# Attention and two feed-forward layers on one core: z and the memory matrices in one load per batch entry, and a new task order

## The chip, the cores and the metric

The kernel runs on one core of one Trainium2 chip. A core has five engines with instruction streams of their own: TensorE (PE; its weight loads are shown apart as PEld), VectorE (DVE), ScalarE (ACT), GpSimd (POOL) and SyncE (SP). SP does no arithmetic here; it issues nearly all the transfers between memory and the core, one after the other. The metric is the time of one execution on the device in microseconds (us), smaller is better.

## The reference

Three parts follow each other. B, H, S, D are 4, 8, 576, 64; M and z are a given memory of each head.

```
scores = q @ k^T / sqrt(D), causal;  a = softmax(scores);  local = a @ v
p = phi(q)                                  # elu(q) + 1
mem = (p @ M) / (p . z + 1e-6)
x = sigmoid(beta) * mem + (1 - sigmoid(beta)) * local     # [B, H, S, D] -> [B*S, H*D]
x = (silu(x @ w_gate) * (x @ w_val)) @ w_out              # 512 -> 1536 -> 512
x = bounded_square(x @ w_in) @ w_out2                     # 512 -> 2048 -> 512
```

## The kernel before

The work is written as tasks (engine, length, priority, what must be done before, which buffers it holds). A planner, `Plan.order`, walks through time with these lengths: whenever an engine is free, it takes the ready task with the lowest priority number whose buffers are free. The order that comes out is written down engine by engine, and on the chip each engine then follows its list strictly; a load that must wait on SP holds up all the loads behind it. There are two plans. The first holds the attention, the decoding of twelve weight tiles and the first products of the feed-forward layer (early units, `L1031`, tile `xh`). The second holds the rest.

The attention goes by pairs of heads: 16 pairs, four of each batch entry, each in `Attention.pair(b, n)`. For one pair the steps are these.

- SP loads `kn` (k, 4 issues: two of 128x4x64 and the two tails), `qn` (q, 3 issues), `vn` (v, 3 issues), z as `zb` (all partitions) and `zh` (two halves) with 3 issues, and the memory matrix `MZ` with 2 issues. `kn`, `vn`, `zb`, `MZ` have three buffers each.
- PE transposes k and q (`tk`, `tm`, `tq`), DVE or ACT copy them out, PE makes the scores (`s`, L611 and L641), DVE takes the maximum (L621, L648), ACT the exponential (L628, L659).
- POOL scales each block of `a` by its sum (L696). PE transposes it (`t`, L707, L730, L747), and DVE or ACT copy the result out as `R`.
- ACT and DVE make phi(q) as `p` (L530, L533, L537); POOL multiplies it by z (L542, L546), folds it (L553), and scales `p` by the norm (L563); PE transposes it (`tp`), and it is copied out as `P`.
- PE adds P @ M (L775) and R @ v (L782) in `av0` and `av1`. The result goes to `x`, and SP stores it.

POOL also does three of the steps of each weight tile (L875, L878, L911). The first early unit can run when a batch entry's first 512 tokens of `x` are stored and loaded again as `xh`.

The priorities are numbers in the tables `ORDER`, `FIRST_ORDER` (the first three pairs), `EARLY`, `GROUP_AT` and `X_AT`; `COPY` says which of DVE and ACT does a copy. The planner counts one issue on SP as 530 ns. Ahead of all, PE runs 16 products of zeros of 64 columns (`hold`, L1132).

The loads that the change touches:

```
def load_z():
    st["zb"] = self.bt.tile([P, 2, D], F32, name="zb", tag="zb")
    nc.sync.dma_start(
        st["zb"].rearrange("p h d -> p (h d)"),
        self.z[b, hs].rearrange("h d -> (h d)").partition_broadcast(P))
    st["zh"] = self.bt.tile([P, D], F32, name="zh", tag="zh")
    for h in range(2):
        nc.sync.dma_start(st["zh"][h * 64:(h + 1) * 64], self.z[b, 2 * n + h].partition_broadcast(64))

def load_M():
    for h in range(2):
        nc.sync.dma_start(MZ()[halves[h], h], self.M[b, 2 * n + h])
```

Of the kernel before, what the change touches and what calls it, by code (L numbers as in the profile page):

```python
# [9 lines left out]
F32 = mybir.dt.float32  # L10
# [20 lines left out]
FIRST_PAIRS = 3  # L31
AB, RB1, RB0 = 3, 2, 2
NOACT = 4
WARM = 16
AHEAD = 30
CUTS = (0, 2, 4)
EARLY = (35250.2957, 41308.3926, 11466.9687, 5162.3933, -48855.3305, 35090.3538, 21413.9511, 24260.6754, 7741.602, 20677.2758, 29371.8961, 20358.7385)
# [7 lines left out]
GROUP_AT, X_AT = (33565.3008, -22387.616, 43473.4923), (39993.454, 16553.201, -28923.1154)  # L45
# [10 lines left out]
HT = 512  # L56
# [8 lines left out]
    "load": -9480.7466, "load_v": 47393.1398, "load_z": -13855.6362, "load_M": 23016.7593, "tk": 27046.2635,  # L65
    "tm": -61762.0282, "tq": -17638.6547, "tk.cp": -18004.5022, "tm.cp": -2334.3136, "tq.cp": 3746.4569,
    "min": -8183.9045, "exp": -8979.6499, "phi": -13315.5241, "w": -36009.8218, "fold": -10020.024, "nrm":
# [9 lines left out]
}  # L77
FIRST_ORDER = {
    "load": -31396.1901, "load_v": 17116.4282, "load_z": -30006.9326, "load_M": 10452.2857, "tk": 47974.63,
    "tm": -14289.6988, "tq": -9446.1095, "tk.cp": -11189.0118, "tm.cp": -15504.3662, "tq.cp": 3520.7596,  # L80
    "min": -24283.9254, "exp": -25956.4452, "phi": 2222.4379, "w": -21034.9661, "fold": -31090.2871, "nrm":
# [9 lines left out]
}  # L91
COPY = {"tk": "ACT", "tm": "DVE", "tq": "ACT", "tp": "DVE", "tp4": "ACT", "t4": "ACT", "t03": "ACT", "t02": "DVE",
        "t01": "ACT", "t13": "DVE", "t12": "ACT", "t11": "ACT"}
# [13 lines left out]
class Plan:  # L107
# [38 lines left out]
    def dma(self, prio, times, fn, deps=(), uses=(), behind=None):  # L146

        t = self.add("SP", 530 * len(times), prio, fn, deps, uses, 0, behind)
        self.last = t
        return self.add("DMA", sum(times), prio, lambda: None, [t], uses)  # L150
# [85 lines left out]
    def emit(self, spare=None, place=None):  # L236

        end, todo = 0, self.order()
        until = max((t["at"] for t in todo if place in t["uses"]), default=0)
        for t in todo:
            if spare and t["eng"] == "PE":
                if end and t["at"] < until:
                    spare(t["at"] - end)
                end = t["at"] + t["dur"]
            t["fn"]()
# [57 lines left out]
class Attention:  # L306
# [3 lines left out]
    def __init__(self, ctx, tc, plan, q, k, v, M_prev, z_prev, beta, cst, xs):  # L310
        self.tc, self.nc, self.plan = tc, tc.nc, plan
        nc = tc.nc
# [3 lines left out]
        pool = lambda name, bufs: ctx.enter_context(tc.tile_pool(name=name, bufs=bufs))  # L316
        self.ld, self.bt, self.ph = pool("ld", 3), pool("bt", 3), pool("ph", 2)
# [3 lines left out]
        for tags, n in ((("kn", "qn", "vn", "zb", "K", "S", "P", "QZ", "MZ"), 3), (("a4",), 2),  # L321
                        (("a0", "a1", "a2", "a3"), AB), (("R1_0", "R1_1"), RB1),
                        (("R0_0", "R0_1"), RB0), (("e", "p", "x"), 2), (("mn",), 3), (("bank",), 8)):
            for t in tags:
                plan.cap(t, n)

        ac = self.ac
# [23 lines left out]
        self.spare = plan.inst("bank")  # L351
        for t in self.a4:
            nc.gpsimd.memset(t[:, S:640], 0.0)
        self.QZ, self.MZ = ([ac.tile([P, 2, D], F32, name=f"{x}_{i}") for i in range(3)] for x in ("QZ", "MZ"))
# [33 lines left out]
    def pair(self, b, n):  # L388
# [42 lines left out]
        i_k, i_q, i_v = pl.inst("kn"), pl.inst("qn"), pl.inst("vn")  # L431
# [24 lines left out]
        i_z, i_M = pl.inst("zb"), pl.inst("MZ")  # L456
        i_K, i_S, i_P, i_Q4 = pl.inst("K"), pl.inst("S"), pl.inst("P"), pl.inst("QZ")
        QZ, MZ = (lambda: self.QZ[i_Q4.slot]), (lambda: self.MZ[i_M.slot])

        def load_z():  # L460
            st["zb"] = self.bt.tile([P, 2, D], F32, name="zb", tag="zb")
            nc.sync.dma_start(
                st["zb"].rearrange("p h d -> p (h d)"),
                self.z[b, hs].rearrange("h d -> (h d)").partition_broadcast(P))
            st["zh"] = self.bt.tile([P, D], F32, name="zh", tag="zh")
            for h in range(2):
                nc.sync.dma_start(st["zh"][h * 64:(h + 1) * 64], self.z[b, 2 * n + h].partition_broadcast(64))

        def load_M():
            for h in range(2):  # L470
                nc.sync.dma_start(MZ()[halves[h], h], self.M[b, 2 * n + h])
# [14 lines left out]
        t_z = dma("load_z", [182, 91, 91], load_z, uses=[i_z])  # L486
        t_M = dma("load_M", [91, 91], load_M, uses=[i_M])


        def mk(kind, shape):  # L490
            if kind not in st:
                st[kind] = self.st.tile(shape, F32, name=kind, tag=kind)
            return st[kind]
# [45 lines left out]
        def f_w():  # L539
            w, p = st["e"], st["p"]  # L540
            zp = st["zb"]
            nc.gpsimd.tensor_mul(  # L542
                w[:, 0:8].rearrange("p (c h) d -> p c h d", h=2),
                p[:, 0:8].rearrange("p (c h) d -> p c h d", h=2),
                zp[:, None, :, :].to_broadcast([P, 4, 2, D]))
            nc.gpsimd.tensor_mul(w[:, 8], p[:, 8], st["zh"])  # L546
# [213 lines left out]
        def av(rg, deps):  # L760
# [3 lines left out]
            i_o = bank()  # L764
# [23 lines left out]
            def lo():  # L788
# [4 lines left out]
                    [i_o, i_P, i_v, i_M, *(i_R1, i_R0)[rg], *([self.spare] if num < FIRST_PAIRS else [])])  # L793
# [242 lines left out]
def tile_attention_two_moe(  # L1036
# [78 lines left out]
    with ExitStack() as actx:  # L1115
# [12 lines left out]
        def hold(n=WARM):  # L1128
            if "t" not in idle:
                idle["t"] = at.ps.tile([P, HT], F32, name="idle", tag=f"bank{at.spare.slot}")  # L1130
            for _ in range(n):
                nc.tensor.matmul(idle["t"][:, 0:P // 2], still, still[:, 0:P // 2], start=True, stop=True)  # L1132

        idle = {}
        plan.add("PE", 10, -2.0e6, hold, uses=[at.spare])
# [458 lines left out]
```

## Time and profile before

| | |
|---|---|
| median of 3 runs | 1071.93 us (1071.68 to 1072.39) |
| profiled execution, its own time | 1074.18 us |
| span of its profile | 1072.4 us |
| PE / PEld busy | 98% / 81% |
| DVE / ACT / POOL busy | 62% / 54% / 20% |
| granted clock of PE, mean | 0.992 |

The span is what the profiler recorded, and the execution's own time is 1.78 us longer. Busy shares are means over the whole span: POOL works in the attention alone, which is the first quarter. A busy PE is not PE at its peak, since the time of a product is that between its start and its modelled end, and products overlap. The granted clock is a share of 2.4 GHz; 0.50 is 1.2 GHz.

### The profile page before, as it was taken

To read this page: it belongs to the slowest core of one execution; us is meant where nothing else is said; L and a number is where in the kernel's file an instruction comes from. 1 tells how busy PE (TensorE), PEld (TensorE's weight loads), DVE (VectorE), ACT (ScalarE), POOL (GpSimd) and SP (SyncE) were. 2 spreads that over 40 slices of the span, in tenths; PEclk is the share of its full clock that TensorE was granted. 3 is DMA by queue.
4 is the path that set the end of the run, shared out by engine and by line. 5 is a ranking of instruction groups with operands and counts; after the bars stand their busy time and mean duration, and the time that the engine had idled before them with its cause. 6 is when DMAs were issued, how large, how long until landed. Compare 5 with 4: busy or idle time off the path is not lost.

```text
span 1072.4 us, 17753 instructions
## 1 busy us (share of the span) xinstructions
PE 1050.2 (98%) x6112; PEld 874.0 (81%) x6112; DVE 666.8 (62%) x1531; ACT 573.8 (54%) x1298; POOL 217.1 (20%) x302
## 2 busy tenths in 40 slices
PE   7989999999999999999999999899999999999998
PEld 6656667767779888889888888788899998899987
DVE  4868877773005787867877677653657577543443
ACT  6868788884212445535445444554555555444443
POOL 6979988993000000000000000000000000000000
PEclk9889999999999999999999999999999999999999
DMA  6577555334486879856985959899887987954522
GB/s 138 125 208 196 162 154 151 98 113 141 167 279 229 283 257 374 301 176 221 343 300 203 365 208 400 331 405 407 313 342 257 396 297 303 390 185 170 177 79 79
DMA packets 178025, 260.71 MB, mean 243 GB/s; under 512 B 74256, under 2 KB 102928, under 8 KB 177936
## 3 DMA queue, kind: packets, MB, share of 16 engines
q1 hardware_dynamic: 176030, 258.23, 69.4%
q10 hardware_dynamic: 1906, 1.35, 0.4%
q8 instruction: 49, 0.80, 0.3%
q14 instruction: 40, 0.33, 0.1%
HBM read 177.74 MB, written 81.79 MB: 242 GB/s over the span
## 4 chain that ended last, share of the span: by engine, by line
PE 93%; SPq 2%; DMA 2%; DVE 1%; ACT 1%; issue 0%; POOL 0%; ACTq 0%; DVEq 0%
PE mm L1031 28%; PE acc L1534 18%; PE mm L1283 16%; PE acc L1378 14%; PE av L782 4%; PE s L611 3%; PE t L730 2%; PE av L775 2%; PE s L641 1%; PE t L747 1%; PE t L707 1%; PE tp L569 1%; SPq L439 1%; DMA vn<-in_v_dram 0%; DMA raw<-in_moe_w_gate_dram 0%; PE tq L511 0%
## 5 line engine op out<-in xcount | busy, mean ns | idle before, releaser
L1534 PE MATMUL acc<-wu,h 128*128 128x512 f32 x864 | 211.9, 393 | 5.0 <-DVE h L1200 4.0
L1031 PE MATMUL mm<-xb,wu 128*128 128x512 f32 (+1 forms) x1008 | 201.3, 359 | 0.0
L1031 PEld LDWEIGHTS mm<-xb,wu 128*128 128x128 f32 x1008 | 170.0, 189 | 28.2
L1534 PEld LDWEIGHTS acc<-wu,h 128*128 128x128 f32 x864 | 157.6, 189 | 35.4 <-DVE h L1200 2.3
L1283 PE MATMUL mm<-xb,wu 128*128 128x256 f32 x1296 | 169.0, 284 | 0.6 <-ACT mm L1354 0.6
L1283 PEld LDWEIGHTS mm<-xb,wu 128*128 128x128 f32 x1296 | 164.9, 192 | 5.0 <-ACT mm L1354 1.0
L1378 PE MATMUL acc<-h,wu 128*128 128x512 f32 (+1 forms) x720 | 151.7, 368 | 0.0
L1378 PEld LDWEIGHTS acc<-h,wu 128*128 128x128 f32 x720 | 125.6, 189 | 22.3
L1197 ACT CAST h<-t 128x512 fp32r<-128x512 f32 (+1 forms) x140 | 80.5, 578 | 77.8 <-DVE t L1273 30.5
L1267 ACT ACTIVATE t<-mm,half 128x512 f32<-128x512 f32 (+1 forms) x80 | 51.6, 646 | 120.8 <-PE mm L1283 73.9
L1200 DVE TENSOR_TENSOR h<-t,h 128x512 fp32r<-128x512 f32 (+1 forms) x140 | 88.1, 635 | 40.6 <-ACT h L1197 39.9
L1031 PE MATMUL mm<-xh,wu 128*128 128x512 f32 x432 | 107.5, 401 | 0.0
L696 POOL TENSOR_SCALAR a<-a,r,OGP 128x512 f32<-128x512 f32 (+4 forms) x144 | 102.1, 719 | 20.2 <-DVE r L687 15.0
L1273 DVE SCALAR_TENSOR_TENSOR t<-mm,t 128x512 f32<-128x512 f32 (+1 forms) x80 | 50.9, 637 | 73.8 <-ACT t L1270 73.8
L1031 PEld LDWEIGHTS mm<-xh,wu 128*128 128x128 f32 x432 | 79.3, 188 | 18.9 <-issue 1.5
L1079 ACT COPY gvo<-mm 128x512 f32<-128x512 f32 (+1 forms) x80 | 43.3, 543 | 93.7 <-PE mm L1031 91.1
L628 ACT ACTIVATE a<-a,mn 128x256 f32<-128x256 f32 (+3 forms) x128 | 71.3, 561 | 14.7 <-DVE mn L621 14.2
L621 DVE CUSTOM_DVE_ANT_0 a<-s,mask 128x256 f32<-128x256 f32 (+3 forms) x128 | 57.7, 484 | 14.7 <-PE s L611 14.3
L848 ACT ACTIVATE wA<-raw 128x512 f32<-128x512 f32 x64 | 42.7, 672 | 34.9 <-DMA raw<-in_moe_w_in_dram 17.7
L782 PE MATMUL av<-R,vn 128*64 128x320 f32 (+4 forms) x448 | 51.1, 360 | 5.1 <-DMA vn<-in_v_dram 5.1
L782 PEld LDWEIGHTS av<-R,vn 128*64 128x64 f32 x448 | 34.0, 138 | 26.6 <-DMA vn<-in_v_dram 6.4
L853 DVE TENSOR_SCALAR wA<-wA 128x512 f32<-128x512 f32 x68 | 34.0, 502 | 30.7 <-ACT wA L848 30.3
(124 smaller groups left out, 1379.6 us busy)
## 6 DMA issues: line engine op xcount, KB each, us to landing
xb<-ys SPq DMA_DIRECT2D x93, 512.0 KB, 7.2
park<-wu SPq DMA_DIRECT2D x40, 512.0 KB, 6.0
wu<-park SPq DMA_DIRECT2D x40, 512.0 KB, 9.2
xb<-xs SPq DMA_DIRECT2D x32, 512.0 KB, 6.9
gv<-gv SPq DMA_DIRECT2D x32, 512.0 KB, 6.0
ys<-yo SPq DMA_DIRECT2D x31, 512.0 KB, 6.9
gv<-gvo SPq DMA_DIRECT2D x60, 256.0 KB, 3.4
raw<-in_moe_w_out_dram SPq DMA_DIRECT2D x28, 512.0 KB, 5.7
```

What stands on the lines that cost most here:

```text
L621: nc.vector.tensor_tensor_reduce(a, st[f"s{h}{c}"][:, 0:kl], self.mask0[:, 512 - kl:512], -0.125, 3.0e38, ALU.add, ALU.min, mn[:, o:o + 1])
L628: nc.scalar.activation(a, a, AF.Exp, bias=mn[:, o:o + 1], scale=-1.0, accum_out=sm[:, o, 0:1])
L696: nc.gpsimd.tensor_scalar(a, a, st["mn"]["r"][:, o:o + 1], self.OGP[:, n, o:o + 1], op0=ALU.mult, op1=ALU.mult)
L782: nc.tensor.matmul(o[halves[h], c0:c1], st["vn"][:, kc, h], r, start=False, stop=i == len(terms) - 1, tile_position=(0, h * 64), skip_grou ...
L1031: nc.tensor.matmul(out, kt_of(unit, pw, kt), x[kt][:, px, cols], start=(kt == 0 and i == 0), stop=(kt == KT - 1 and i == 2))
L1197: nc.scalar.copy(s["h"][:, 0], s["t"])
L1200: nc.vector.tensor_sub(s["h"][:, 1], s["t"], f32(s["h"][:, 0]))
L1267: nc.scalar.activation(mk_t(o), src(), AF.Relu, bias=half, scale=0.5)
L1273: nc.vector.scalar_tensor_tensor(o["t"], src(), 1.0, o["t"], op0=ALU.max, op1=ALU.min)
L1283: nc.tensor.matmul(out, pair["k"](k, pw, j), y["x"][piece][:, px, j], start=first and not (i or j), stop=last and j == 1 and i == 2, skip_ ...
L1378: nc.tensor.matmul(state[m][:, 0:n], l, r, start=(begin and i == 0), stop=(end and i == 2), skip_group_check=True)
L1534: nc.tensor.matmul(state[m], s["h"][:, px, m * P:(m + 1) * P], unit["w"][:, pw], start=(begin and i == 0), stop=(end and i == 2), skip_gro ...
```

## The change

z and M are loaded once for a batch entry, by the first of its four pairs: `zb` and `MZ` get a dimension over the four pairs, and 3 + 2 issues serve four pairs where 4 x (3 + 2) did. The tiles for z, M and `P` have two buffers instead of three. The planner counts an issue in the first plan as 600 ns instead of 530 (`self.over` is set there alone). All the tables of priorities are new, and `COPY` moves some copies between ACT and DVE. The products of zeros are 8 of 128 columns instead of 16 of 64, and they stand ahead of the plan; `hold` and the arguments of `emit`, which nothing used, are gone.

```diff
-WARM = 16
+WARM = 8
...
 ORDER = {
-    "load": -9480.7466, "load_v": 47393.1398, "load_z": -13855.6362, "load_M": 23016.7593, "tk": 27046.2635,
+    "load": -13097.6716, "load_v": 55113.6308, "load_z": -18855.7456, "load_M": 38998.1826, "tk": 51026.1438,
...
-COPY = {"tk": "ACT", "tm": "DVE", "tq": "ACT", "tp": "DVE", "tp4": "ACT", "t4": "ACT", "t03": "ACT", "t02": "DVE",
-        "t01": "ACT", "t13": "DVE", "t12": "ACT", "t11": "ACT"}
+COPY = {"tk": "DVE", "tm": "ACT", "tq": "ACT", "tp": "ACT", "tp4": "ACT", "t4": "DVE", "t03": "ACT", "t02": "ACT",
+        "t01": "DVE", "t13": "DVE", "t12": "ACT", "t11": "ACT"}
...
-        t = self.add("SP", 530 * len(times), prio, fn, deps, uses, 0, behind)
+        t = self.add("SP", (600 if self.over else 530) * len(times), prio, fn, deps, uses, 0, behind)
...
-        for tags, n in ((("kn", "qn", "vn", "zb", "K", "S", "P", "QZ", "MZ"), 3), (("a4",), 2),
+        for tags, n in ((("kn", "qn", "vn", "K", "S", "QZ"), 3), (("zb", "MZ", "a4", "P"), 2),
...
-        i_z, i_M = pl.inst("zb"), pl.inst("MZ")
+        if n == 0:
+            self.batch = {"z": pl.inst("zb"), "M": pl.inst("MZ")}
+        held = self.batch
+        i_z, i_M = held["z"], held["M"]
...
-        QZ, MZ = (lambda: self.QZ[i_Q4.slot]), (lambda: self.MZ[i_M.slot])
+        QZ, MZ = (lambda: self.QZ[i_Q4.slot]), (lambda: self.MZ[i_M.slot][:, n])
...
         def load_z():
-            st["zb"] = self.bt.tile([P, 2, D], F32, name="zb", tag="zb")
+            held["zb"] = self.bt.tile([P, NP, 2, D], F32, name="zb", tag="zb")
             nc.sync.dma_start(
-                st["zb"].rearrange("p h d -> p (h d)"),
-                self.z[b, hs].rearrange("h d -> (h d)").partition_broadcast(P))
-            st["zh"] = self.bt.tile([P, D], F32, name="zh", tag="zh")
+                held["zb"].rearrange("p n h d -> p (n h d)"), self.z[b].rearrange("h d -> (h d)").partition_broadcast(P))
+            held["zh"] = self.bt.tile([P, NP, D], F32, name="zh", tag="zh")
             for h in range(2):
-                nc.sync.dma_start(st["zh"][h * 64:(h + 1) * 64], self.z[b, 2 * n + h].partition_broadcast(64))
+                nc.sync.dma_start(
+                    held["zh"][halves[h]],
+                    self.z[b].rearrange("(n h) d -> h n d", h=2)[h].partition_broadcast(64))
...
             for h in range(2):
-                nc.sync.dma_start(MZ()[halves[h], h], self.M[b, 2 * n + h])
+                nc.sync.dma_start(
+                    self.MZ[i_M.slot][halves[h], :, h, :], self.M[b].rearrange("(n h) p d -> h p n d", h=2)[h])
...
-        t_z = dma("load_z", [182, 91, 91], load_z, uses=[i_z])
-        t_M = dma("load_M", [91, 91], load_M, uses=[i_M])
+        if n == 0:
+            held["t_z"] = dma("load_z", [728, 182, 182], load_z, uses=[i_z])
+            held["t_M"] = dma("load_M", [364, 364], load_M, uses=[i_M])
+        t_z, t_M = held["t_z"], held["t_M"]
...
-            for _ in range(n):
-                nc.tensor.matmul(idle["t"][:, 0:P // 2], still, still[:, 0:P // 2], start=True, stop=True)
...
+        idle = at.ps.tile([P, HT], F32, name="idle", tag="bank7")
+        for _ in range(WARM):
+            nc.tensor.matmul(idle[:, 0:P], still, still, start=True, stop=True)
```

In the order of SP, these are the issues of the kernel before that end with the v of the second pair (`vn_1_198`); 73 issues stand ahead of the first of them.

```order
L462 DMA zb_756<-in_z_prev_dram 128x128
L467 DMA zh_758<-in_z_prev_dram 64x64 x2
L462 DMA zb_784<-in_z_prev_dram 128x128
L467 DMA zh_786<-in_z_prev_dram 64x64 x2
L439 DMA kn_1_195<-in_k_dram 128x4x64 x2
L447 DMA kn_1_195<-in_k_dram 64x2x64
L451 DMA kn_1_195<-in_q_dram 64x2x64
L439 DMA kn_2_196<-in_k_dram 128x4x64 x2
L447 DMA kn_2_196<-in_k_dram 64x2x64
L451 DMA kn_2_196<-in_q_dram 64x2x64
L439 DMA vn_1_198<-in_v_dram 128x4x64 x2
L447 DMA vn_1_198<-in_v_dram 64x2x64
```

In the changed kernel, the stretch of SP's order from the v of the first pair (`vn_0_197`) to that of the second is this; 50 issues stand ahead of it.

```order
L429 DMA vn_0_197<-in_v_dram 128x4x64 x2
L437 DMA vn_0_197<-in_v_dram 64x2x64
L429 DMA qn_640<-in_q_dram 128x4x64 x2
L444 DMA qn_640<-in_q_dram 128x1x64
L429 DMA kn_1_195<-in_k_dram 128x4x64 x2
L437 DMA kn_1_195<-in_k_dram 64x2x64
L441 DMA kn_1_195<-in_q_dram 64x2x64
L429 DMA qn_687<-in_q_dram 128x4x64 x2
L444 DMA qn_687<-in_q_dram 128x1x64
L455 DMA zb_719<-in_z_prev_dram 128x512
L459 DMA zh_721<-in_z_prev_dram 64x4x64 x2
L429 DMA vn_1_198<-in_v_dram 128x4x64 x2
```

Before, 64 issues stood ahead of `vn_0_197` and 87 ahead of `vn_1_198`; now they are 50 and 66. Five issues for a batch entry's z and M stand where each pair had its own.

The second place is POOL's first work in the attention. Before, it begins with a step of the first weight tile (`wS`, which needs ACT's `wL`), and the products with z of the first two pairs come third and sixth.

```order
L875 TENSOR_TENSOR wS_357<-wL_362,wS_357 128x512
L878 TENSOR_TENSOR wA_305<-wA_305,wS_357 128x512
L542 TENSOR_TENSOR e_316<-p_333,zb_326 128x512
L546 TENSOR_TENSOR e_316<-p_333,zh_328 128x64
L911 TENSOR_TENSOR wu_431<-wA_305,wu_431 128x512
L553 TENSOR_TENSOR e_316<-e_316 128x9x32
L542 TENSOR_TENSOR e_355<-p_384,zb_347 128x512
L546 TENSOR_TENSOR e_355<-p_384,zh_349 128x64
L553 TENSOR_TENSOR e_316<-e_316 128x9x16
L553 TENSOR_TENSOR e_355<-e_355 128x9x32
L696 TENSOR_SCALAR a2_392<-a2_392,r_319,OGP_187 128x384
```

In the changed kernel it begins with the first pair's product with z.

```order
L539 TENSOR_TENSOR e_302<-p_325,zb_269 128x512
L543 TENSOR_TENSOR e_302<-p_325,zh_271 128x64
L872 TENSOR_TENSOR wS_332<-wL_336,wS_332 128x512
L550 TENSOR_TENSOR e_302<-e_302 128x9x32
L875 TENSOR_TENSOR wA_296<-wA_296,wS_332 128x512
L539 TENSOR_TENSOR e_343<-p_364,zb_269 128x512
L543 TENSOR_TENSOR e_343<-p_364,zh_271 128x64
L908 TENSOR_TENSOR wu_425<-wA_296,wu_425 128x512
L693 TENSOR_SCALAR a2_372<-a2_372,r_308,OGP_187 128x384
```

The first scaled block of `a` (L696 before, L693 now) is POOL's eleventh step before and its ninth now; two folds moved behind it.

## Rows read from the trace of the kernel before

**Rows 1.** The page, part 1: busy us, share of the span, instructions

```profile
PE 1050.2 (98%) x6112; PEld 874.0 (81%) x6112; DVE 666.8 (62%) x1531; ACT 573.8 (54%) x1298; POOL 217.1 (20%) x302
```

**Rows 2.** Stretches of the span: length, busy us by engine, granted clock, DMA share, GB/s

```profile
core 0: us, PE busy (x) PEld busy (x) DVE busy (x) ACT busy (x) POOL busy (x), PEclk, DMA share, GB/s
0.00:25.00 25.00, 19.30 (x92) 15.62 (x92) 11.92 (x50) 15.35 (x38) 14.99 (x52) 1.00 0.63 142
25.00:50.00 25.00, 23.83 (x150) 16.86 (x149) 19.82 (x71) 20.85 (x62) 22.43 (x32) 0.86 0.55 136
50.00:75.00 25.00, 19.95 (x126) 13.43 (x125) 16.45 (x52) 16.46 (x50) 17.22 (x19) 0.86 0.67 173
75.00:100.00 25.00, 24.83 (x178) 17.09 (x175) 21.63 (x71) 22.84 (x66) 23.23 (x30) 1.00 0.77 203
100.00:200.00 100.00, 100.00 (x688) 70.44 (x688) 74.71 (x246) 82.75 (x237) 90.15 (x110) 1.00 0.59 164
```

**Rows 3.** Timeline of PE, 43 to 100 us: start, length, instruction, idle before

```profile
43.37 0.65 PE L775 MATMUL av<-P,MZ 128*64 128x256 f32 x4
...
54.70 0.65 PE L775 MATMUL av<-P,MZ 128*64 128x256 f32 x4 [0.15 <-DVE mn L621]
60.25 2.21 PE L782 MATMUL av<-R,vn 128*64 128x256 f32 x8 [4.89 <-DMA vn<-in_v_dram]
...
66.66 0.65 PE L775 MATMUL av<-P,MZ 128*64 128x256 f32 x4
67.14 0.82 PE L782 MATMUL av<-R,vn 128*64 128x256 f32 x8
...
77.05 1.13 PE L611 MATMUL s<-K,S 64*128 64x512 f32 x4
...
79.02 0.92 PE L611 MATMUL s<-K,S 64*128 64x256 f32 x8
...
80.68 0.92 PE L611 MATMUL s<-K,S 64*128 64x384 f32 x4
...
98.99 0.60 PE L569 MATMUL tp<-ident,p 128*128 128x128 f32 x4
99.43 0.27 PE L572 MATMUL tp<-ident,p 128*64 128x128 f32 x1
```

**Rows 4.** Two stretches for PE alone: busy us, granted clock, DMA share, GB/s

```profile
28.00:32.00 4.00, 4.00 (x17) 0.50 0.42 97
60.00:64.00 4.00, 3.75 (x16) 0.50 0.91 246
```

**Rows 5.** Timeline of PE, 5 to 27 us

```profile
7.93 0.42 PE L505 MATMUL tm<-ident,kn 128*128 128x128 f32 x1
...
24.51 0.63 PE L511 MATMUL tq<-ident,qn 128*128 128x128 f32 x4 [1.47 <-DMA qn<-in_q_dram]
25.93 0.90 PE L730 MATMUL t<-ident,a 128*128 128x128 f32 x3 [0.80 <-POOL a L696]
```

**Rows 6.** Timeline of SP's queue: start, issue time, issues

```profile
0.74 1.01 SPq L439 DMA_DIRECT2D kn<-in_k_dram  x2
...
13.45 1.16 SPq L467 DMA_DIRECT2D zh<-in_z_prev_dram  x2
...
20.80 1.08 SPq L439 DMA_DIRECT2D qn<-in_q_dram  x2
...
41.09 1.22 SPq L439 DMA_DIRECT2D vn<-in_v_dram  x2
...
57.69 1.14 SPq L439 DMA_DIRECT2D vn<-in_v_dram  x2
```

**Rows 7.** DMA issues, 0 to 110 us: count, KB each, median us to landing

```profile
vn<-in_v_dram SPq DMA_DIRECT2D x14, 128.0 KB, 2.6
```

**Rows 8.** Timeline of POOL, 14 to 27 us

```profile
16.01 1.28 POOL L875 TENSOR_TENSOR wS<-wL,wS 128x512 f32<-128x512 f32 x1 [8.31 <-ACT wL L872]
...
25.23 0.65 POOL L696 TENSOR_SCALAR a<-a,r,OGP 128x384 f32<-128x384 f32 x1
```

**Rows 9.** Timeline of DVE, 12 to 13 us

```profile
12.44 0.75 DVE L537 SCALAR_TENSOR_TENSOR p<-qn,e 128x576 f32<-128x576 f32 x1
```

More of the change, by code (lines that the diff above doesn't have):

```diff
@@ L33 @@
 NOACT = 4
-WARM = 16
+WARM = 8
 AHEAD = 30
 CUTS = (0, 2, 4)
-EARLY = (35250.2957, 41308.3926, 11466.9687, 5162.3933, -48855.3305, 35090.3538, 21413.9511, 24260.6754, 7741.602, 20677.2758, 29371.8961, 20358.7385)
+EARLY = (58464.4906, 31703.8921, 46024.3389, 15376.5891, -67113.9713, 33679.2323, 24516.8779, 64604.3348, 926.9641, 15791.9914, 50392.9186, 34533.2938)
 XH, GVO = 4, 3
@@ L43 @@
 PHASES = (2, 3, 3)
-GROUP_AT, X_AT = (33565.3008, -22387.616, 43473.4923), (39993.454, 16553.201, -28923.1154)
+GROUP_AT, X_AT = (58101.0278, -5262.7152, 78550.5678), (81713.5868, 13183.1344, -54614.9227)
 FIRST = (0, 8, 1, 2, 9, 3, 4, 10, 5, 6, 11, 7)
@@ L64 @@
 ORDER = {
-    "load": -9480.7466, "load_v": 47393.1398, "load_z": -13855.6362, "load_M": 23016.7593, "tk": 27046.2635,
-    "tm": -61762.0282, "tq": -17638.6547, "tk.cp": -18004.5022, "tm.cp": -2334.3136, "tq.cp": 3746.4569,
-    "min": -8183.9045, "exp": -8979.6499, "phi": -13315.5241, "w": -36009.8218, "fold": -10020.024, "nrm":
[9 rows of a table removed]
+    "load": -13097.6716, "load_v": 55113.6308, "load_z": -18855.7456, "load_M": 38998.1826, "tk": 51026.1438,
+    "tm": -96571.9864, "tq": -19483.9254, "tk.cp": -45495.7399, "tm.cp": -7125.2447, "tq.cp": -15756.7918,
+    "min": -42893.5849, "exp": -31473.534, "phi": 250.0948, "w": -55573.7784, "fold": -2977.3896, "nrm":
[9 rows of a table added]
 }
 FIRST_ORDER = {
-    "load": -31396.1901, "load_v": 17116.4282, "load_z": -30006.9326, "load_M": 10452.2857, "tk": 47974.63,
-    "tm": -14289.6988, "tq": -9446.1095, "tk.cp": -11189.0118, "tm.cp": -15504.3662, "tq.cp": 3520.7596,
-    "min": -24283.9254, "exp": -25956.4452, "phi": 2222.4379, "w": -21034.9661, "fold": -31090.2871, "nrm":
[9 rows of a table removed]
-}
-COPY = {"tk": "ACT", "tm": "DVE", "tq": "ACT", "tp": "DVE", "tp4": "ACT", "t4": "ACT", "t03": "ACT", "t02": "DVE",
-        "t01": "ACT", "t13": "DVE", "t12": "ACT", "t11": "ACT"}
+    "load": -35369.7195, "load_v": 11324.0126, "load_z": -39943.6113, "load_M": -1948.6302, "tk": 57244.7662,
+    "tm": -20365.3582, "tq": 43517.0557, "tk.cp": -28665.4259, "tm.cp": -32651.252, "tq.cp": -2666.435, "min":
+    -17582.8303, "exp": -34662.1945, "phi": 32542.1117, "w": -33941.3334, "fold": -21505.6005, "nrm":
[9 rows of a table added]
+}
+COPY = {"tk": "DVE", "tm": "ACT", "tq": "ACT", "tp": "ACT", "tp4": "ACT", "t4": "DVE", "t03": "ACT", "t02": "ACT",
+        "t01": "DVE", "t13": "DVE", "t12": "ACT", "t11": "ACT"}
 def f32(ap):
@@ L234, in order, with emit @@
         return out
[L236 to L247, printed above, removed]
+    def emit(self):
+        for t in self.order():
             t["fn"]()
@@ L316, in __init__ @@
         pool = lambda name, bufs: ctx.enter_context(tc.tile_pool(name=name, bufs=bufs))
-        self.ld, self.bt, self.ph = pool("ld", 3), pool("bt", 3), pool("ph", 2)
+        self.ld, self.bt, self.ph = pool("ld", 3), pool("bt", 2), pool("ph", 2)
         self.st, self.ap, self.at = pool("st", 3), pool("ap", AB), pool("at", 1)
@@ L350, in __init__ @@
             nc.gpsimd.memset(t[64:128, 4], 0.0)
-        self.spare = plan.inst("bank")
         for t in self.a4:
             nc.gpsimd.memset(t[:, S:640], 0.0)
-        self.QZ, self.MZ = ([ac.tile([P, 2, D], F32, name=f"{x}_{i}") for i in range(3)] for x in ("QZ", "MZ"))
+        self.QZ = [ac.tile([P, 2, D], F32, name=f"QZ_{i}") for i in range(3)]
+        self.MZ = [ac.tile([P, NP, 2, D], F32, name=f"MZ_{i}") for i in range(2)]
         for t in self.QZ + self.MZ:
@@ L485, in pair @@
             "vn", lambda: self.vn[i_v.slot], lambda t: t[:, 0:4], self.v, tail_half), uses=[i_v])
-        t_z = dma("load_z", [182, 91, 91], load_z, uses=[i_z])
-        t_M = dma("load_M", [91, 91], load_M, uses=[i_M])
+        if n == 0:
+            held["t_z"] = dma("load_z", [728, 182, 182], load_z, uses=[i_z])
+            held["t_M"] = dma("load_M", [364, 364], load_M, uses=[i_M])
+        t_z, t_M = held["t_z"], held["t_M"]
         def mk(kind, shape):
             if kind not in st:
-                st[kind] = self.st.tile(shape, F32, name=kind, tag=kind)
+                st[kind] = (self.ph if kind == "P" else self.st).tile(shape, F32, name=kind, tag=kind)
             return st[kind]
@@ L540, in f_w @@
             w, p = st["e"], st["p"]
-            zp = st["zb"]
+            zp = held["zb"][:, n]
             nc.gpsimd.tensor_mul(
@@ L545, in f_w @@
                 zp[:, None, :, :].to_broadcast([P, 4, 2, D]))
-            nc.gpsimd.tensor_mul(w[:, 8], p[:, 8], st["zh"])
+            nc.gpsimd.tensor_mul(w[:, 8], p[:, 8], held["zh"][:, n])
         def f_nrm():
@@ L792, in av @@
             t = add("PE", c_two(w, *cols), name, f, deps + t_P + [l_v, t_M],
-                    [i_o, i_P, i_v, i_M, *(i_R1, i_R0)[rg], *([self.spare] if num < FIRST_PAIRS else [])])
+                    [i_o, i_P, i_v, i_M, *(i_R1, i_R0)[rg]])
             t = add("ACT", c_act(w), name + ".hi", hi, [t], [i_o, i_x])
@@ L1127, in tile_attention_two_moe @@
         plan.cap("gvo", GVO), plan.cap("xh", XH)
-        def hold(n=WARM):
-            if "t" not in idle:
-                idle["t"] = at.ps.tile([P, HT], F32, name="idle", tag=f"bank{at.spare.slot}")
-            for _ in range(n):
-                nc.tensor.matmul(idle["t"][:, 0:P // 2], still, still[:, 0:P // 2], start=True, stop=True)
-        idle = {}
-        plan.add("PE", 10, -2.0e6, hold, uses=[at.spare])
+        idle = at.ps.tile([P, HT], F32, name="idle", tag="bank7")
+        for _ in range(WARM):
+            nc.tensor.matmul(idle[:, 0:P], still, still, start=True, stop=True)
         for (kind, f), prio in zip(ready, EARLY):
```

36 rows, old and new, of tables (FIRST_ORDER, ORDER) are left out of this document.

## The prediction

> **What bounds the kernel now.** I read the page's busy shares first: PE is busy 1050.2 of 1072.4 us [rows 1], so 22.2 us of idle time is all that waits can hold. The stretches of 25 us say where: 5.70, 1.17, 5.05 and 0.17 us lie in the first 100 us, 12.1 together, and from 100 to 200 there is none [rows 2]. The other 10.1 us come later, where the orders of the two kernels end alike on each engine but POOL, which is done by then. Work on PE is the same in both but for the products of zeros, so the time changes by what PE loses early: idle time, and time at the lower clock. The clock is seen in the same view (0.86 from 25 to 75 us [rows 2]), and closer by in [rows 4]: 0.50, so 1.2 GHz, from 28 to 32 and from 60 to 64 us, where PE is busy throughout or nearly.
>
> The timeline of PE names the largest loss. At 55.4 us PE is ready for the v of the second pair and stands 4.89 us until 60.25 [rows 3]. Behind this wait the clock is low: the eight products that take 0.82 us at 67.14 take 2.21 us at 60.25 [rows 3]. SP's queue shows why v is late: it is issued at 57.69 [rows 6], and 2.6 us to landing [rows 7] gives 60.3, when PE goes on. Nothing but its turn held it: 87 issues stand ahead of it in the order, and (57.69 - 0.74) / 87 is 0.655 us each; for the first pair's v, (41.09 - 0.74) / 64 is 0.63. SP goes back to back, and the place in its queue sets the time.
>
> **The change, part by part.** *Fewer issues.* 20 transfers for z and M remain of 80. Ahead of the first pair's v stand 50 issues, so it is issued at 0.74 + 50 x 0.63 = 32.2 and lands at 34.8. Ahead of the second's stand 66: 0.74 + 66 x 0.655 = 44.0, landed 46.6, against 60.3.
>
> A transfer for four pairs has more pieces, and no row shows one. The nearest: two `zh` issues of 64x64 take 1.16 us, two `qn` issues of 128x4x64, eight times as many pieces, 1.08 [rows 6]. So I take an issue at the same price; the other end, price by pieces, is a rival below.
>
> *When PE needs v.* The first transposes of `a` wait for POOL, at 25.93 [rows 5], and POOL started at 16.01 because its first task needed ACT's `wL` [rows 8]. Now it starts with the product of z, for which `p` is there at 12.44 + 0.75 = 13.2 [rows 9]; 2.8 us earlier at most, nothing at least, since `wS` and `wu` still wait for ACT. I take 2: first transposes at 24. From there to the first `av`, PE took 43.37 - 25.93 = 17.4 us [rows 3, 5] for 63 transposes and 18 score products; now 51 and 12 stand there. At four fifths that is 13.9, so 37.9, behind the v landed at 34.8. From the first `av` to the second pair's, it took 54.70 - 43.37 = 11.3 us [rows 3]; two transposes (0.11 each, 98.99 to 99.43 for four) and two score products (0.8) fewer make 10.3, and with the 0.5 us that the M part takes before v (66.66 to 67.14), PE wants this v at 48.7. It has landed for 2 us: the wait is gone.
>
> *What that is worth.* PE reaches this point at 48.7 instead of 60.25, 11.55 us earlier, but has done less: by the order, 14 transposes (1.5 us) and one chunk of score products (1.06 to 1.13, 0.92 and 0.92 us, less their overlaps 2.7 [rows 3]) come later, 4.2 us. That leaves 7.35. The low clock behind the wait goes too: 60.25 to 66.66 is 6.41 us for eight v products and 20 transposes, which at the later pace are 0.82 + 20 x 0.11 = 3.0, so 3.4. Sum 10.75.
>
> *What is late next: POOL.* It idles 2.57, 7.78 and 1.77 us from 25 to 100 [rows 2], 12.1 in all. If it starts 2.8 earlier and never idles, PE could gain 14.9 before POOL binds. At its idle share from 100 to 200, 9.85%, 64 us of work hold 6.3 us of idle, and the gain would be 8.6. PE bounds that stretch and POOL need not idle so much, so I keep near the row of the wait itself: 10.7.
>
> *Costs at nothing.* Copies that change engines move some 448 columns a pair from ACT to DVE, about 0.6 us by [rows 9] (576 columns 0.75), 3 us over five pairs; DVE idles 17.1 us between 25 and 100 [rows 2], which covers it, and without that cover it is 3 us. The third batch entry's z waits for a tile until the fourth pair's product with z; by POOL's list that is near 35 to 38 us, and SP comes to it at 0.74 + 63 x 0.655 = 42. M's tile is the slower rival below. `P` with two tiles waits for the `av` of two pairs ahead, which stand earlier on PE. The products of zeros end earlier by up to 2 us (first transposes at 7.93 [rows 5], k landed at about 5.9 by its 4 issues and 2.6 us); POOL's start hangs on q, not on k, so I take 0 and keep 2 for the range.
>
> The profiled execution took 1074.18 us, 1.78 more than its span and 2.25 more than the median of the runs; I carry the difference to the median: 1071.93 - 10.7 = **1061.2 us**.
>
> **The rivals.** *A: the wait comes back, shorter (20%).* SP may itself wait for `qn` tiles, which come free only when phi of the third and fourth pairs is done; both stand just ahead of the second pair's v. If that holds v up by 6 us, PE waits 4 and restarts at the low clock for another 3.4: 10.7 - 7.4 = 3.3, so 1068.6. For it: the row of `qn` at 24.51, 1.47 us idle [rows 5], shows loads of q arriving late. Against it: SP reaches them at about 34 and 39 us.
>
> *B: more than the wait goes (13%).* The low clock at 28 to 32 us [rows 4] may vanish as well, some 3 us, and the start come 2 us earlier: up to 15.7, so 1056.2. It needs POOL without any idle time, which no row shows.
>
> *C: the bundles cost as much as what they replace (5%).* If issue time goes by pieces, six `zh` and two `M` issues ahead of the second v cost four times as much: 8 x 3 x 0.6 = 14.4 us, v is issued at 58.4, later than now, and the time stays near 1072. The Trainium skill speaks for that: Perfetto Trace Analysis, section What "DMA-bound" means, says that solid slices on an issuing sequencer are descriptor generation, and that only larger descriptors help there. By it the sum would be nothing, since `zh` and M keep pieces of 256 bytes. The rows of `zh` and `qn` above contradict it.
>
> *D: slower (7%).* M now has two tiles for four batch entries. The third entry's M, 113 issues down SP's list, comes up at 0.74 + 113 x 0.655 = 75 us and waits until the fourth pair's `av` is done, by PE's order about 82. Behind it stand the seventh pair's v and the loads of `xh` that feed the early units. Each us that the fourth pair is late past what PE can fill is a us lost; it decides when the fill is 10.7 + 2.1 us short, and at 14 us the time is 1075. Against it: that v is needed some 30 us later, and the x store behind M needs the same `av` anyway.
>
> **How the numbers follow.** The forecast holds 55% with a range of its own from 1058.5 (POOL idles little) to 1065. A measurement of this kernel tells about 0.2%, 2.1 us, from no change. Faster: forecast, A, B, 88%. Same: C, 5%. Slower: D, 7%. The range goes from B's 1056 to 1070, a little past A, and leaves out C, D and the tails.
>
> **What would show it.** PE's wait for `vn` near 49 us under 1 us, and no stretch at clock 0.50 behind 50 us; the second v issued near 44; SP with gaps before 110 us; `zh` and M issues near 0.6 us; the first early unit (L1028) near 74 to 77 us; PE's idle time in the first 100 us near 6 instead of 12.1. I am wrong if that wait is back elsewhere with the same length, if bundled issues take over 1.5 us, or if POOL, without idle time from 25 to 75, makes PE wait.

## The result and the profile after

The changed kernel takes 1063.66 us (median of 4 runs, 1063.30 to 1064.51) where the kernel before, on the same chip, takes 1072.16 (1071.68 to 1073.72): a ratio of 0.9919, 95% interval 0.9902 to 0.9937, so 8.5 us less. Two later measurements of the same pair gave 0.9934 [0.9922, 0.9947] and 0.9929 [0.9910, 0.9948], 7.4 and 7.7 us less. The forecast was 10.7 less.

Part 1 of the page of the changed kernel, beside [rows 1]:

```profile
PE 1042.1 (98%) x6096; PEld 864.2 (81%) x6096; DVE 671.5 (63%) x1547; ACT 570.6 (54%) x1282; POOL 215.9 (20%) x301
```

The span is 1061.6 us, so PE idles 19.5 us; before it was 22.2. PE is also busy for 8.1 us less, with the same products but for the zeros. The stretches, with the columns of [rows 2]:

```profile
0.00:25.00 25.00, 19.66 (x89) 14.02 (x91) 13.49 (x47) 16.34 (x45) 18.29 (x55) 1.00 0.69 168
25.00:50.00 25.00, 21.51 (x152) 14.43 (x151) 18.70 (x67) 21.78 (x66) 21.95 (x29) 0.93 0.76 178
50.00:75.00 25.00, 24.88 (x184) 16.76 (x184) 23.54 (x81) 23.18 (x68) 23.77 (x30) 1.00 0.92 245
75.00:100.00 25.00, 24.80 (x171) 16.37 (x168) 23.41 (x74) 21.35 (x63) 22.23 (x30) 1.00 0.45 118
```

Compare the third row with that of before: PE went from 19.95 to 24.88 us busy and the clock from 0.86 to 1.00. The second row went the other way, from 23.83 to 21.51: idle time came into a stretch that had little. PE's timeline, with the columns of [rows 3], says what stands in each place:

```profile
6.27 0.45 PE L502 MATMUL tm<-ident,kn 128*128 128x128 f32 x1 [1.44 <-DMA kn<-in_q_dram]
...
22.47 0.49 PE L727 MATMUL t<-ident,a 128*128 128x128 f32 x3
...
34.55 0.55 PE L727 MATMUL t<-ident,a 128*128 128x128 f32 x3 [1.57 <-POOL a L693]
...
37.50 1.24 PE L772 MATMUL av<-P,MZ 128*64 128x320 f32 x4 [1.56 <-ACT P L415]
38.52 3.49 PE L779 MATMUL av<-R,vn 128*64 128x320 f32 x20
...
48.02 0.65 PE L772 MATMUL av<-P,MZ 128*64 128x256 f32 x4
48.50 0.82 PE L779 MATMUL av<-R,vn 128*64 128x256 f32 x8
...
51.51 2.23 PE L779 MATMUL av<-R,vn 128*64 128x320 f32 x20
...
73.08 1.64 PE L1028 MATMUL mm<-xh,wu 128*128 128x512 f32 x6
```

The row at 48.50 answers to the one at 60.25 before: eight products with the second pair's v, no wait ahead of them, 0.82 us instead of 2.21. Two new waits stand at 34.55 and 37.50, the second for ScalarE's copy of `P`. Behind them the 20 products at 38.52 take 3.49 us where the same 20 take 2.23 at 51.51. That is the clock (length, PE busy, granted clock, DMA share, GB/s):

```profile
28.00:32.00 4.00, 3.66 (x28) 1.00 0.48 102
32.00:36.00 4.00, 2.37 (x16) 1.00 0.83 226
36.00:40.00 4.00, 2.50 (x10) 0.70 0.97 172
40.00:44.00 4.00, 4.00 (x31) 0.87 0.63 163
60.00:64.00 4.00, 3.88 (x33) 1.00 0.97 246
```

Both stretches of [rows 4] are at full clock now; instead part of 36 to 44 us is at 1.2 GHz. SP's queue, with the columns of [rows 6]:

```profile
5.16 1.26 SPq L459 DMA_DIRECT2D zh<-in_z_prev_dram  x2
...
30.57 1.25 SPq L465 DMA_DIRECT2D MZ<-in_M_prev_dram  x2
31.87 0.60 SPq L840 DMA_DIRECT2D raw<-in_moe_w_gate_dram  x1
32.52 1.05 SPq L429 DMA_DIRECT2D vn<-in_v_dram  x2
...
42.64 1.15 SPq L429 DMA_DIRECT2D vn<-in_v_dram  x2
...
84.28 1.31 SPq L465 DMA_DIRECT2D MZ<-in_M_prev_dram  x2
```

A `zh` or M issue for four pairs takes 0.59 to 0.63 us in the first 160 us, but for two of 0.94 and 1.38; v is issued at 32.52 and 42.64 instead of 41.09 and 57.69. It lands 3.2 us later, by the view of DMA issues from 0 to 110 us, which answers to [rows 7] (2.6); the first pair's v takes 4.2 us and lands near 37 us, where PE multiplies with it from 38.52:

```profile
vn<-in_v_dram SPq DMA_DIRECT2D x16, 128.0 KB, 3.2
```

### The profile page after: what moved, and what is told of

It reads as the page before. It is cut to its first block, busy times and chain, and to the rows that moved or that the text cites. A ratio compares the mean times of both kernels' runs of the same rounds, so it can differ in the third digit from the quotient of the medians.

```text
span 1061.6 us, 17557 instructions
## 1 busy us (share of the span) xinstructions
PE 1042.1 (98%) x6096; PEld 864.2 (81%) x6096; DVE 671.5 (63%) x1547; ACT 570.6 (54%) x1282; POOL 215.9 (20%) x301
## 4 chain that ended last, share of the span: by engine, by line
PE 93%; ACT 3%; DVE 1%; POOL 1%; issue 1%; DMA 0%; SPq 0%; DVEq 0%; POOLq 0%
PE mm L1028 28%; PE acc L1526 18%; PE mm L1275 16%; PE acc L1370 14%; PE av L779 4%; PE s L608 4%; PE t L727 2%; PE av L772 2%; PE s L638 1%; PE t L744 1%; ACT a L625 1%; PE t L704 1%; POOL a L693 1%; PE tp L566 1%; PE tk L497 1%
## 5 line engine op out<-in xcount | busy, mean ns | idle before, releaser
L693 POOL TENSOR_SCALAR a<-a,r,OGP 128x512 f32<-128x512 f32 (+3 forms) x144 | 98.8, 698 | 11.1 <-DVE r L684 7.0
L415 DVE COPY R<-t 128x256 f32<-128x256 f32 (+3 forms) x96 | 35.8, 417 | 43.3 <-PE t L744 37.0
L845 ACT ACTIVATE wA<-raw 128x512 f32<-128x512 f32 x64 | 42.8, 672 | 34.5 <-DMA raw<-in_moe_w_in_dram 16.1
L779 PEld LDWEIGHTS av<-R,vn 128*64 128x64 f32 x448 | 32.8, 139 | 22.4 <-issue 2.0
L779 PE MATMUL av<-R,vn 128*64 128x320 f32 (+4 forms) x448 | 50.0, 363 | 0.0
```

The source lines that it names most:

```text
L693: nc.gpsimd.tensor_scalar(a, a, st["mn"]["r"][:, o:o + 1], self.OGP[:, n, o:o + 1], op0=ALU.mult, op1=ALU.mult)
L779: nc.tensor.matmul(o[halves[h], c0:c1], st["vn"][:, kc, h], r, start=False, stop=i == len(terms) - 1, tile_position=(0, h * 64), skip_grou ...
```

## The experiments

**Theory Q:** the gain comes from the place of v in SP's queue, so fewer issues ahead of it are enough. **Theory O** (first rival): the new task order brings a good part. Four kernels take the change apart. The first has the order of before with z and M bundled. Its edit to the kernel before (there are also 15 products of zeros instead of 16, fed from a tile that was there, to make room):

```diff
+            if "zb" in held:
+                return
+            held["zb"] = self.bt.tile([P, NP, 2, D], F32, name="zb", tag="zb")
...
+            if "M" in held:
+                return
+            held["M"] = True
...
-                nc.sync.dma_start(MZ()[halves[h], h], self.M[b, 2 * n + h])
+                nc.sync.dma_start(
+                    self.MZ[b % 2][halves[h], :, h, :], self.M[b].rearrange("(n h) p d -> h p n d", h=2)[h])
```

> The kernel before, its order kept task by task on every engine, with z and M loaded once per batch entry (60 issues fewer). To make room the zeros for the first products come from the mask tile, and 15 products of 64 columns stand there instead of 16. Theory Q (the place in SP's queue): 68 issues instead of 87 stand ahead of the second pair's v, so it is issued at 0.74 + 68 x 0.655 = 45.3 us and has landed by 48.5; PE wants it at 55.4, so the wait of 4.89 us and the low clock behind it (3.4) go: 8.3 us less than before, about 1063.8. Theory O (the new order of tasks does it): less than 3 us gained, over 1069.

It took 1065.29 us, ratio 0.9932 [0.9920, 0.9945], 8.0 us less than before in that measurement (1073.25): nearly the whole gain without the new order. SP issues the two v at 33.62 and 46.95, and PE finds the second one there:

```profile
25.96 0.90 PE L741 MATMUL t<-ident,a 128*128 128x128 f32 x3 [4.02 <-POOL a L707]
...
54.52 0.65 PE L786 MATMUL av<-P,MZ 128*64 128x256 f32 x4 [0.15 <-DVE mn L632]
55.00 0.82 PE L793 MATMUL av<-R,vn 128*64 128x256 f32 x8
```

PE reaches this v at 55.00 as in the order of before (55.4), against 48.50 in the changed kernel, yet the time is the same within 2 us. Of these 6.5 us the prediction had already put down 4.2 to products that the new order only does later. What the old order lacks is GpSimd's early start: its 4.02 us of wait at 25.96 answer to the 0.80 at 25.93 in [rows 5], with k and q there earlier.

The changed order with single transfers (z is split in the same way; ratios in this section are all to the kernel before):

```diff
...
-            for h in range(2):
-                nc.sync.dma_start(
-                    self.MZ[i_M.slot][halves[h], :, h, :], self.M[b].rearrange("(n h) p d -> h p n d", h=2)[h])
+            for m in range(NP):
+                for h in range(2):
+                    nc.sync.dma_start(self.MZ[i_M.slot][halves[h], m, h], self.M[b, 2 * m + h])
```

> The changed kernel, its order kept on every engine, but each load of z and M split into the transfers of before: 12 issues where 3 stand, 8 where 2 stand. Theory Q: 74 instead of 50 issues ahead of the first v (issued at about 49, landed 52, wanted at 38) and 99 instead of 66 ahead of the second (issued at 65.6, landed 68.5, wanted at 48.5): about 20 us of waits and one or two stretches at the low clock, 1083 to 1092. Theory O: the order carries the gain, and splitting costs under 3 us, below 1067.

1084.45 us, 1.0115 [1.0099, 1.0131]: slower than before. PE's timeline shows the wait for v back, and more than that: the three waits for k up to 32 us hold 11 us, and PE waits 5.13 us for the copy of `P`, ahead of which a weight step on ScalarE waits 3.94 us for its load.

```profile
53.72 3.73 PE L779 MATMUL av<-R,vn 128*64 128x320 f32 x20
...
67.08 1.99 PE L779 MATMUL av<-R,vn 128*64 128x256 f32 x8 [2.96 <-DMA vn<-in_v_dram]
```

The new order lives on bundled issues. Theory O falls. M alone bundled at the old order (the part of the first diff behind its "..."; the zeros as before) takes four issues from ahead of each v:

> The kernel before, its order kept, with M alone loaded once per batch entry. Theory Q: 83 instead of 87 issues ahead of the second v, issued at 55.1, landed 57.7 to 58.3: PE still waits 2.3 to 2.9 us and then still runs at the low clock, so 2 to 2.6 us are gained, 1069.5 to 1070.2. Theory O: no change, 1072.

1069.28 us, 0.9968 [0.9955, 0.9980], 4 us less, where 2 to 2.6 were expected. The wait shrinks, from 4.89 us [rows 3] to what follows, and the clock from 25 to 75 us is 0.93 instead of 0.86:

```profile
57.06 2.06 PE L790 MATMUL av<-R,vn 128*64 128x256 f32 x8 [1.98 <-DMA vn<-in_v_dram]
```

Over the five kernels the second v goes out where its place in the list says, at 0.63 to 0.68 us an issue:

| | issues ahead of the second v | issued, us | PE waits for it, us |
|---|---|---|---|
| new order, single | 99 | 62.69 | 2.96 |
| before | 87 | 57.69 | 4.89 |
| old order, M bundled | 83 | 54.43 | 1.98 |
| old order, both bundled | 68 | 46.95 | 0 |
| changed | 66 | 42.64 | 0 |

The first row waits less than the second because PE itself comes to this place later there (64.1 instead of 55.4 us).

The fourth is the changed kernel with the zeros of before:

```diff
-WARM = 8
+WARM = 16
...
-            nc.tensor.matmul(idle[:, 0:P], still, still, start=True, stop=True)
+            nc.tensor.matmul(idle[:, 0:P // 2], still, still[:, 0:P // 2], start=True, stop=True)
```

> The changed kernel with 16 products of zeros of 64 columns at the start, as before, instead of 8 of 128. PE's first transposes move from 6.27 to about 8 us. If the start of PE counts, the time rises by 1.5 us, to 1065.2; if the chain at the start hangs on q, ACT and POOL, it stays within 0.5 us of 1063.7. If the shorter zeros have cost something in clock, it falls.

1065.37 us, 0.9929 [0.9915, 0.9942], 7.9 us less than before: within what the changed kernel itself gave (7.4 to 8.5). From 24 to 70 us its PE timeline is the same, 1.1 to 1.5 us later, the wait for `P` too (38.87 instead of 37.50, both 1.56 us). So the shorter zeros bring PE forward by that much at most; on the clock it was not told from nothing.

A second set, with the changed kernel again, adds the short zeros to the old order (on top of the first kernel):

```diff
-WARM = 15
+WARM = 8
...
-                nc.tensor.matmul(idle["t"][:, 0:P // 2], still, still[:, 0:P // 2], start=True, stop=True)
+                nc.tensor.matmul(idle["t"][:, 0:P], still, still, start=True, stop=True)
```

> The changed kernel itself once more, so that the three kernels beside it are compared on one chip. Both theories expect 1062.5 to 1065 us and 8 to 9.5 us less than the kernel before.

> The kernel with the old task order, z and M bundled (1065.29 us), and now also the 8 wide products of zeros at the start in place of 15 narrow ones. That is every part of the change except the new order. Theory Q (the place in SP's queue, and next to it the shorter zeros) expects the two gains to add: 8.0 and about 1.2, so 1063.5 to 1064.5 us, equal to the changed kernel within 0.2%. Theory O (the new task order brings a part of the gain) expects this kernel to stay at 1065 us or above, 1.5 us or more behind the changed one.

The changed kernel took 1065.65 us, the old order with bundles and short zeros 1065.30, ratio 0.9922 [0.9908, 0.9936] against 0.9934. Equal, as theory Q said of the pair; its 1063.5 to 1064.5 was too low, since the zeros added nothing that can be told.

Then the question was why 8 and not 10.7. **Theory W:** the wait for the copy of `P` and the clock behind it eat 2 to 3 us. Its rival: v is nearly as late, and a wait of the same size takes its place. One task is moved in the list that the planner puts out:

```diff
-    def emit(self):
-        for t in self.order():
+    def emit(self, moves=()):
+        todo = self.order()
...
-            plan.emit()
+            plan.emit([('tp4.cp', 0, 'tp.cp', 0)])
```

> The changed kernel with one task moved: ScalarE copies the last 64 columns of the first pair's P right behind the first 512, at about 32.4 us instead of 37.0. Theory W (the forecast was 2.2 us too good because TensorE's own wait of 1.56 us for this copy and the low clock of 0.70 behind it eat it) expects the wait at 37.5 to go, the first products with v (3.49 us for 20) to take about 2.3, and 2 to 3 us less than the changed kernel: 1060.7 to 1061.7 us. The rival, that the time comes back at once because v lands only at about 36 us or because the scaled copies of the scores come up to 0.9 us later, expects a new wait of the same size near 38 us and less than 0.7 us of gain.

1064.57 us, 0.9924 [0.9912, 0.9936]: 1.1 us less than the changed kernel beside it, less than the intervals can tell. The wait for `P` is gone, as W said, and a shorter one for v, as the rival said, is there instead (its lines are six higher, L785 is L779):

```profile
36.19 0.76 PE L778 MATMUL av<-P,MZ 128*64 128x320 f32 x4
37.70 2.96 PE L785 MATMUL av<-R,vn 128*64 128x320 f32 x20 [0.75 <-DMA vn<-in_v_dram]
```

The next kernel has GpSimd's scaling ahead as well, by one more entry in that list:

```diff
-            plan.emit([('tp4.cp', 0, 'tp.cp', 0)])
+            plan.emit([('tp4.cp', 0, 'tp.cp', 0), ('w', 2, 't02.sc', 1)])
```

> As the kernel with the P copy moved, and in addition GpSimd scales the 384-column block of the second pair's scores ahead of the third product with z instead of behind it, so that TensorE's wait of 1.57 us at 34.5 us shrinks to about 0.5. Theory W expects about 1 us less again, 1059.7 to 1060.8 us, or half of it where v (issued at 32.5, landed near 36) then is what comes last. The rival expects no further gain, since GpSimd idles about 0.9 us longer for the row sums and its later scalings come up to 1.1 us later, where TensorE then waits.

1065.68 us, 0.9935 [0.9923, 0.9947], no gain. The wait at 34.5 shrank to 0.73, and v took all of it:

```profile
33.97 0.55 PE L733 MATMUL t<-ident,a 128*128 128x128 f32 x3 [0.73 <-POOL a L699]
...
38.59 2.93 PE L785 MATMUL av<-R,vn 128*64 128x320 f32 x20 [2.54 <-DMA vn<-in_v_dram]
```

W's price does not show in these times: the first pair's v, issued at 33.26 us and 33.99 in these two, lands some 4.5 us later and so is late by nearly as much as `P`. The profiles do not settle it. At the same products near 680 us the kernel with the `P` copy moved is 2.8 us ahead of the changed one beside it (677.55 and 680.33), as W forecast, but the changed kernel's first profile is there at 677.58 too; and behind that place the clock fell in the first of these three and not in the others (last section). The changed kernel of this set shows that the copy of `P` itself hangs on SP's queue. On ScalarE a weight step stands ahead of it and waits for its load:

```profile
38.34 0.67 ACT L845 ACTIVATE wA<-raw 128x512 f32<-128x512 f32 x1 [1.64 <-DMA raw<-in_moe_w_gate_dram]
38.91 0.86 ACT L415 COPY P<-tp 64x64 f32<-64x64 f32 x4
```

That load was issued at 33.43 us here and at 31.87 in the first profile, where the step waited for nothing; PE's wait for `P` was 3.12 here and 1.56 there. So the last set moves v forward too, by an entry that puts four issues for a later k behind v: alone, with that for `P`, and with both others. **Theory V:** the copy of `P` and v are two waits in a row at one place, so v alone gains nothing, and both moves together 2 to 4 us. The edit to `emit` is as above, with loads found by name on SP.

```diff
-            plan.emit()
+            plan.emit([('load', 10, 'load_v', 0)])
```

> The changed kernel on the chip of the three kernels beside it: 1063 to 1066 us by every theory.

> The changed kernel with one task moved in SP's queue: the four issues of a k load that TensorE needs only past 40 us now stand behind the first pair's v, which is issued some 2.4 us earlier. Theory V (the copy of P and v are two waits in a row at one place, so that either alone gives little) expects no gain: TensorE still waits for the copy of P, 1.5 to 3 us near 37 to 39 us, and the time stays within 1 us of the changed kernel. The rival, that the place in SP's queue alone still sets the end here, expects 2 us less.

> Both moves together, v 2.4 us earlier and the copy of P right behind its first part. Theory V expects no wait for P nor for v near 36 to 39 us, and 2 to 4 us less than the changed kernel (1.5 to 3.1 us of wait and about 1.2 us of low clock). The rival expects another wait of the same length right behind, for scaled scores, and less than 1 us of gain.

> The two moves and the scaling of the 384-column block ahead of the product with z, which cut the wait near 34.5 us from 1.5 to 0.73 us but had v waited for by 2.54 us at its old place. Theory V expects the v wait gone (2.4 us earlier) and 0.5 to 1 us less than with the two moves. The rival expects no difference from the kernel with the two moves.

| kernel | us | ratio to before | where PE waits over 1 us, 30 to 55 us |
|---|---|---|---|
| changed | 1065.47 (1064.87 to 1066.83) | 0.9929 [0.9910, 0.9948] | scaled `a` 1.56, `P` 2.17 |
| v earlier | 1064.82 (1063.58 to 1066.63) | 0.9924 [0.9904, 0.9944] | scaled `a` 1.49, `P` 1.34 |
| v earlier, `P` first | 1065.53 (1063.26 to 1067.31) | 0.9926 [0.9906, 0.9945] | scaled `a` 1.48, second pair's v 2.23 |
| v, `P`, scaling | 1063.39 (1063.20 to 1064.80) | 0.9909 [0.9889, 0.9930] | a copy of `R` 1.26 |

v alone brings nothing, as V said. The two together clear 35 to 40 us, and then the second pair's v is late: it is issued at 43.67, and its loads land 4.1 us behind their issues (median), where 2.9 were enough in the first profile of the changed kernel:

```profile
48.00 1.36 PE L785 MATMUL av<-R,vn 128*64 128x256 f32 x8 [2.23 <-DMA vn<-in_v_dram]
```

V's 2 to 4 us did not come there. With all three moves PE is fed better from 32 to 44 us, and the clock is whole:

```profile
32.00:36.00 4.00, 3.06 (x24) 1.00 1.08 245
36.00:40.00 4.00, 3.23 (x31) 1.00 0.66 150
40.00:44.00 4.00, 3.87 (x32) 1.00 0.62 161
```

That kernel is 2.1 us below the changed one beside it, and no run of the one reaches a run of the other; but the intervals overlap and it was measured once. The first measurement of the changed kernel gave 0.9919 [0.9902, 0.9937] with a span of 1061.6 us, against 0.9909 and 1061.4 here. So a gain over the changed kernel is not shown.

## Why the prediction was right, and where its sum was off

**Fewer issues: right.** 32.2 and 44.0 us were forecast for v, 32.52 and 42.64 measured, at the price of a single issue. The landing was forecast too short for the first pair: 2.6 us, where it took 4.2. M alone at the old order confirms the dose: part of the issues, part of the wait.

**When PE needs v: right in place, wrong in what sets it.** First transposes of `a` at 24 (22.47), first `av` at 37.9 (37.50), second pair's v at 48.7 (48.50), without a wait. The second of these is in part luck. The 13.9 us between the first two were scaled from a stretch of 17.4 us that ran in part at 0.50 [rows 4], and were taken as work alone. The low clock did not come there, and 15.0 us were measured, of which 1.57 are a wait for GpSimd, 1.56 one for `P` and 0.34 one for a copy of `R`; the first transposes came 1.5 us early.

**What it is worth: mechanism right, sum 2 to 3 us too high.** Three profiles of the changed kernel stand beside the one of before, whose execution took 1074.18 us, 2.25 more than the median it was set against:

| | before | changed, three profiles |
|---|---|---|
| span | 1072.4 | 1061.6, 1064.4, 1063.6 |
| PE idle in the first 100 us | 12.1 | 9.2, 11.0, 10.5 |
| PE idle behind | 10.1 | 10.3, 10.4, 10.4 |
| PE busy | 1050.2 | 1042.1, 1043.0, 1042.7 |

The idle time, forecast at 6, is the term that was mis-sized: it fell by 1 to 3 us and not by 6. The 4.89 us are gone, and waits for k near 6 us (1.44 in the first profile), for scaled `a` (1.57) and for `P` (1.56) have come. PE's busy time fell by 7.2 to 8.1 us: the zeros take 3.79 us where they took 7.09, 3.3 less. What is left, 3.9 to 4.8, is not all the clock behind the wait, which was forecast at 3.4: some 1.5 us of it lie near 690 us, where the profile of before has a stretch at 1.2 GHz (granted clock 0.63 from 688 to 692 us) that these three do not have and that the change does not touch (last section). The forecast's own list did not add up either: 6.1 us less idle and 3.4 of clock make 9.5, not 10.7.

**The clock: half right.** No 0.50 is left behind 50 us, and the low stretch at 28 to 32 went as well, which was part of rival B. But 0.70 came up at 36 to 40 (0.65 and then 0.50 up to 44 us in the third profile), behind the two new waits.

**POOL: right that it was near, wrong that it would bind by its load.** It idles 3.05 us from 25 to 50 [second row of the stretches], and still a block comes 1.57 us late, because of its place behind the products with z. The bound that the step worked out from POOL's idle share, 8.6 us, and set aside came nearest to the 8.5: POOL idles 7.05 of the 75 us from 25 to 100. But behind 25 us PE waits for POOL only these 1.57 us, so that POOL set the gain is not shown.

**Costs at nothing.** The copies' load on DVE was covered. What the step did not look at is their order on ScalarE: the last 64 columns of `P` stand behind exponentials and a weight step, 5 us after their transposes. Taking the zeros as 0 stands: the profiles show PE some 1.3 us earlier, the times nothing.

**The rivals.** A did not come: SP was never held up enough for the second v to be late. A wait of 2.23 us for it came when the two waits ahead were taken away, but by another way than A's: v was issued 1.0 us later than in the changed kernel, and took 1.2 us more to land. C is refuted by the rows: 0.59 to 0.63 us for nearly every issue with four times the pieces. The Trainium skill's Perfetto Trace Analysis, section What "DMA-bound" means, names larger descriptors as the help where an issuing sequencer is solid; the runs disagree for this queue: with M alone bundled the pieces stayed at 256 bytes, four issues fewer stood ahead of each v, and the time fell by 4 us. D's mechanism is in the trace (the third entry's M goes out at 84.28, 75 and 82 were forecast) and cost nothing: PE does not wait for it. The first early unit came at 73.08, a little before the 74 to 77.

## What to carry to other kernels

Where a queue's issues run back to back, as SP's do here at 0.63 to 0.68 us each, a load's time is its place in that list: count the issues ahead and price each, and bundling loads that share a source moves everything behind it. Price the landing from its own spread (2.6 us in the median of v before, up to 4.8 us in the second profile of the changed kernel), not from one median. A wait that goes uncovers the next: here `P`, then the first v, then the second v lay within 1 to 3 us of each other, and moving `P` or the first v alone gave nothing that could be measured. Make idle time and busy time add up to the forecast separately, look for a low clock outside the changed stretch too, and read more than one profile of the same kernel before pricing 2 us.

## What was not expected of the hardware

Now and then an issue on SP takes longer than its like. In each profile of the changed kernel, as it is or with tasks moved, one between 26 and 28 us took 0.5 to 1.6 us longer. In the changed kernel of the second set it was this one, 2.10 us where such an issue takes 0.60:

```profile
26.78 2.10 SPq L437 DMA_DIRECT2D kn<-in_k_dram  x1
```

The weight load behind it went out 1.56 us later than in the first profile, which had a milder one (1.51 for two). That may be much of what sets two runs of one kernel apart by 2 to 3 us; its cause stays open.

The clock did not follow the length of a wait. In the changed kernel it was 0.70 from 36 to 40 us, behind two waits of 1.6 us. In the kernel with the `P` copy and the scaling moved it stayed at 1.00 there, with a wait of 2.54 us. In the second plan, at 677 to 699 us by kernel, every profile has the same wait of 2.02 or 2.03 us; behind it the clock fell to 1.2 GHz for a few us in six of fourteen profiles (the kernel before, the old order with both bundled, the zeros as before, and three with tasks moved) and stayed whole in the others, the three of the changed kernel among them. Here are the changed kernel and the one with the `P` copy moved:

```profile
677.58 1.62 PE L1526 MATMUL acc<-wu,h 128*128 128x512 f32 x6 [2.03 <-DVE h L1192]
679.03 3.04 PE L1275 MATMUL mm<-xb,wu 128*128 128x256 f32 x24
...
677.55 2.07 PE L1532 MATMUL acc<-wu,h 128*128 128x512 f32 x6 [2.03 <-DVE h L1198]
679.42 4.14 PE L1281 MATMUL mm<-xb,wu 128*128 128x256 f32 x24
```

They come to this place together, and their spans are 1061.6 and 1063.1 us. In the second the clock is 0.82 from 676 to 680 us and 0.76 from 680 to 684, in the first 1.00. So 1.5 us between two profiles can be this alone, and what decides it is open.

Sixteen products of zeros with 64 columns took 7.09 us, eight with 128 columns 3.79: 0.44 and 0.47 us each, so half the width saved next to nothing.
